# Where a weight-splitting step stands between the products of a sequence mixer, and at the start of an MLP

## The chip, the core and the metric

The kernel runs on one core of one Trainium2 chip. The metric is device time in microseconds (us), the median of several runs. The engines are TensorE (PE in the profile, its weight loads PEld), VectorE (DVE), ScalarE (ACT), GpSimd (POOL) and SyncE (SP); SyncE and ScalarE also issue DMAs from their own queues, in their program's order.

## The reference

Two layers of the same kind run one after the other on x (2048 tokens, 576 features). Each layer is a Fourier mixing and then an MLP (576 to 4608 to 576), both behind two layer norms and with a residual:

```python
def _A_ref(x, dft_seq_re, dft_seq_im, dft_hid_re, dft_hid_im):
    a = jnp.einsum("bsd,ed->bse", x, dft_hid_re)
    b = jnp.einsum("bsd,ed->bse", x, dft_hid_im)
    return jnp.einsum("ts,bse->bte", dft_seq_re, a) - jnp.einsum("ts,bse->bte", dft_seq_im, b)

def _B_ref(x, w1, b1, w2, b2):
    h = _gelu(jnp.einsum("bsd,df->bsf", _layernorm(x), w1) + b1)
    return jnp.einsum("bsf,fd->bsd", h, w2) + b2

x = x + _A_ref(_layernorm(x), ...)
x = x + _B_ref(_layernorm(x), ...)
# and both once more
```

Both layers use the same matrices.

## The kernel before

All large products are done in a 2x2 block scheme with seven block products in the place of eight (numbered 1 to 7, run in `ORDER`, 1, 6, 2, 5, 7, 3, 4). To keep fp32 accuracy each operand is split into a high part (fp32r) and a low part (the rest), and each product is three passes, high x high, high x low, low x high. A high part is a ScalarE copy (`activation` with Copy), a low part a VectorE subtraction of it from the source; L201 is the helper `sub`, L198 the helper `add`.

**Sequence** multiplies along the tokens: sixteen t blocks, of which the first two are done in `first_mms` and the other fourteen (t = 2 to 15) in `run`, seven products of 24 matmuls (128x288) each, 98 product steps. In product step n the program issues `low` of step n + 2 on VectorE, `high` of step n + 3 on ScalarE, the 24 matmuls, and `post`, which takes the finished bank away (ScalarE for products 1, 2, 5 and 7, VectorE for 6, 3 and 4, after 4 also the transpose L208; after 7 GpSimd does two adds). `sums(t + 1)` makes two sums of the blocks of the next t on VectorE: `tmp` = block 2 + block 3, and block 2 - block 0. The blocks come in by SyncE's DMAs from `in_cs`, in the order 0, 2, 3, 1, each as a ring buffer falls free (`load_c`). `low` of product 1 also rewrites block 0 (L704), and the next `high`, that of product 6, reads what it wrote.

**The weights' background.** `weights()` is a generator that splits the first MLP matrix, in 18 quarters of seven weight steps. Weight step n is `high(n)` (two ScalarE copies, L284 and L285), `low(n)` (a 128x384 VectorE subtraction, and in four of the seven steps a GpSimd add or subtraction), and `keep(n)`: the store to `w1_parts` and, in four of the seven, the load of the next piece (SyncE). Three stage buffers go round. The Sequence of the first layer advances the generator with `pump()` twice behind a product, and it issues the store on ScalarE's queue there; the MLP's first half goes on with it (`BEHIND` lists at which positions of a group), and its stores are SyncE's.

**MLP** runs over the two halves of the tokens. `inner(q)` makes seven products of seven matmuls (128x512) for one of 18 pieces of the hidden features, `outer` multiplies back (128x288); a group g is two inner runs and the outer products of the group before. `advance()` counts positions in a group and runs what is due there. In the first half of the first layer `make(g)` splits the second MLP matrix beside it; its steps are `one`, `six`, `five`, `three`, `seven`, `four` and `two`, each a ScalarE copy of the high part (L1169) and a VectorE low part (128x576) with the store behind it. Group 0 has no outer products: its positions 0 to 6 are the second half of `inner(0)`, 7 to 13 are `inner(1)`.

All three engines run in program order, and the order is written by hand: there is no scheduler.

Of the kernel before, what the change touches and what calls it, by code (L numbers as in the profile page):

```python
# [15 lines left out]
P = 128  # L16
NT = S // P
DH = D // 2
NP = NT // 2
NQ = F // P // 2  # L20
NG = NQ // 2
# [41 lines left out]
EARLY_X = (12800, 9344, 8192)  # L63
EARLY_T = 10496
BEHIND = (0, 2, 2, 4, 5, 6, 15, 16, 16, 17, 17, 19, 21, 21)
H_AT = (8704, 22400)
C2_AT = (OWN_AT, 37760)
Y_AT = (RN - Y_N, 0)
# [92 lines left out]
def spectral_mixer(ctx: ExitStack, tc: tile.TileContext, x, dh, c0, cs, w1, b1, w2, b2, out):  # L161
# [35 lines left out]
    def add(engine, dst, a, b, op=OP.add):  # L197
        engine.tensor_tensor(dst, a, b, op=op)  # L198
# [65 lines left out]
    def weights():  # L264
        b = raw(4, 3 * P)
        a22, a21, a11, a12 = (b[:, k] for k in range(4))
        g = nc.gpsimd
        steps = ((4, a22, lambda: add(g, a22, a21, a22)), (1, a11, lambda: sub(g, a21, a11, a21)),
                 (5, a22, lambda: sub(g, a11, a22, a11)), (2, a12, lambda: sub(g, a12, a12, a11)),
                 (6, a11, None), (7, a21, None), (3, a12, None))  # L270

        def load(q, k):
            if q < NQ:
                dma(b[:, k], w1[q][:, k])

        def at(n):
            return stage(3, 5 * P)[:, n % 3]

        def cut(a):
            return a.rearrange("p (k f) -> p k f", f=P)  # L280

        def high(n):
            src, t = cut(steps[n % 7][1]), cut(at(n))
            nc.scalar.activation(t[:, 1:4:2], src[:, 0:3:2], AF.Copy)  # L284
            nc.scalar.activation(t[:, 2], src[:, 1], AF.Identity, bias=power[:, 2:3], scale=middle)  # L285

        def low(n):

            q, k = divmod(n, 7)
            i, src, then = steps[k]  # L290
            t = cut(at(n))
            sub(nc.vector, t[:, 0:5:2], cut(src), t[:, 1:4].bitcast(F32))
            if then:
                then()

        def keep(n):

            q, k = divmod(n, 7)
            stores[0].dma_start(w1s[q, steps[k][0] - 1], at(n).bitcast(F32))
            if k in (2, 4, 5, 6):  # L300
                load(q + 1, {2: 0, 4: 2, 5: 1, 6: 3}[k])
            if k == 6:
                made[0] = q + 1

        for k in range(4):
            load(0, k)
        for _ in range(4):
            yield
        high(0)
        for n in range(7 * NQ):  # L310
            yield
            low(n)
            if n + 1 < 7 * NQ:
                high(n + 1)
            yield
            keep(n)
        stage.free()
        raw.free()

# [10 lines left out]
    class Sequence:  # L330
# [354 lines left out]
        def block(self, t, k):  # L685
            return self.live[t, k](NP, P)

        def sums(self, t):
            add(nc.vector, self.tmp(NP, P), self.block(t, 2), self.block(t, 3))
            sub(nc.vector, self.block(t, 2), self.block(t, 2), self.block(t, 0))  # L690

        def source(self, t, i):
            return self.tmp(NP, P) if i == 5 else self.block(t, {1: 0, 6: 0, 2: 1, 7: 2, 3: 1, 4: 3}[i])
# [64 lines left out]
        def run(self, hidden):  # L758
# [12 lines left out]
            for n, (t, i) in enumerate(steps):  # L771
                self.load_c()
                if n and n + 2 < len(steps):
                    self.low(*steps[n + 2])
                if n % 7 == 2 and t + 1 < NT:
                    self.sums(t + 1)
                self.load_c()
                if n + 3 < len(steps):
                    self.high(*steps[n + 3])
                self.mms(t, i)  # L780
                if n == 1:
                    self.first_turn(0, outs[0])
                    hidden.reserve()
                self.post(t, i)
                if n == 1:
                    self.first_post(1, outs[1])
                if n == 3:
                    self.first_turn(1, outs[1])
                if t == NT - 1:
                    hidden.begin(self, ORDER.index(i))  # L790
                if n == 3 and not self.early:
                    dma(b1t, b1)
                if n % 7 != 2 and n > 3 and (t < NT - 1 or n % 7 < 4):
                    pump()
                    pump()
            for k in range(2):
                self.L[k].free()
# [323 lines left out]
    def mlp(hid, store, first, ends, before, after):  # L1121


        half, X, Y = hid.half, hid.X, hid.Y
        stores[0] = nc.sync
        xv, y = X(2, NP, DH), Y(7, 5, TC)
        U = Block(A, U_AT[half], 4 * DH)
        uv = U(4, DH)
# [65 lines left out]

        def advance(to=None):
            at[1] += to is None
            for _ in range(BEHIND.count(at[0]) if to is None and group[0] else 0):
                pump()
            while kept and kept[0][0] <= at[1]:
                kept.pop(0)[1]()  # L1200
            while due and due[0][0] <= (at[0] if to is None else to):
                due.pop(0)[1]()
            at[0] += 1
# [176 lines left out]
        for k in range(4 * first):  # L1380
            load_raw(0, k)
        for g in range(NG + 1):
            at[0], group[0] = 0, g or not first
            if first and not g:
                soon, late = make(0)
                due.extend((n, step) for n, (_, step) in zip((3, 4), soon))
            elif first:
                due.extend(late)
                if g < NG:
                    soon, late = make(g)  # L1390
                    due.extend(soon)
# [117 lines left out]
```

## Time and profile before

| | |
|---|---|
| median of 3 runs | 2625.3 us (2624.54 to 2627.97) |
| the profiled execution | 2624.75 us, span 2623.0 us |
| busy: TensorE, weight loads, VectorE, ScalarE, GpSimd | 2614.4, 2466.3, 1836.8, 1120.2, 791.5 us |
| first layer's Sequence, products | about 60 to 378 us of the span |
| first layer's MLP, first half | from about 440 us |
| second layer's Sequence | about 1320 to 1700 us |

Times in the trace are us from the start of the span. An engine's row gives start, length, engine, line, operation, what it writes and reads with the sizes, a count where neighbours are merged, and in brackets the idle time before it and what ended it. TensorE's row in the page counts pipelined matmuls, so its 100% says that it is seldom empty, not that it runs at its best pace.

### The profile page before, as it was taken

What the parts mean: (1) busy time and instruction counts of PE and PEld (TensorE: products, weight loads), DVE (VectorE), ACT (ScalarE), POOL (GpSimd) and SP (SyncE); (2) the same over time, 40 slices, a digit from 0 to 9 for tenths busy, and PEclk for the clock granted to TensorE, in tenths of its full rate; (3) what the DMA queues carried; (4) which work ended last, traced back from release to release, by engine and by line L of the source; (5) the groups of instructions that cost most, each with busy time, mean ns of one, the idle gap of its engine ahead of it and who ended that gap; (6) DMA issues with size and microseconds to landing.
All of it is one profiled execution on the core that took longest, in us unless ns stands there. A gap on an engine that the chain in (4) does not pass through costs nothing.

```text
span 2623.0 us, 44794 instructions
## 1 busy us (share of the span) xinstructions
PE 2614.4 (100%) x17252; PEld 2466.3 (94%) x17252; DVE 1836.8 (70%) x2580; ACT 1120.2 (43%) x1821; POOL 791.5 (30%) x638
## 2 busy tenths in 40 slices
PE   9999999999999999999999999999999999999999
PEld 9999999899999989998999999999999999899998
DVE  8999987778787765556687776576555557655555
ACT  7555555555553443333354333353333325433332
POOL 5334333544444332222251000132122233322222
PEclk9999999999999999999999999999999999999999
DMA  6667676778788666676544343756666685666664
GB/s 226 223 236 234 234 255 215 266 278 301 279 299 300 178 202 195 194 222 210 173 175 135 122 124 124 211 159 194 193 195 194 195 268 169 199 195 195 194 194 155
DMA packets 223238, 544.91 MB, mean 208 GB/s; under 512 B 23712, under 2 KB 74912, under 8 KB 222880
## 3 DMA queue, kind: packets, MB, share of 16 engines
q1 hardware_dynamic: 210496, 513.91, 62.2%
q10 hardware_dynamic: 12528, 28.12, 2.8%
q8 instruction: 137, 2.24, 0.3%
q14 instruction: 77, 0.63, 0.1%
HBM read 429.87 MB, written 114.72 MB: 208 GB/s over the span
## 4 chain that ended last, share of the span: by engine, by line
PE 92%; DVE 5%; DMA 1%; issue 1%; POOL 1%; ACT 0%; DVEq 0%; ACTq 0%; SPq 0%; POOLq 0%
PE bank L211 91%; DVE R L201 3%; DVE A L201 1%; DMA w_parts<-R 1%; DMA A<-in_cs 0%; PE bank L991 0%; DVE A L198 0%; PE bank L1035 0%; DVE moments L242 0%; PE bank L994 0%; ACT R L698 0%; DMA A<-in_w 0%; DMA R<-w_parts 0%; PE bank L1045 0%; POOL A L198 0%
## 5 line engine op out<-in xcount | busy, mean ns | idle before, releaser
L211 PE MATMUL bank<-R 128*128 128x288 f32 (+2 forms) x16972 | 2585.9, 314 | 3.9 <-DVE R L201 1.2
L211 PEld LDWEIGHTS bank<-R 128*128 128x128 f32 x16972 | 2434.8, 189 | 150.8 <-DVE R L201 4.3
L198 DVE TENSOR_TENSOR A<-bank,A 128x576 f32<-128x576 f32 (+3 forms) x812 | 567.6, 707 | 510.2 <-PE bank L211 457.7
L201 POOL TENSOR_TENSOR R<-A,R 128x512 fp32r<-128x512 f32 (+1 forms) x292 | 380.0, 1310 | 912.4 <-ACT R L1299 560.6
L201 DVE TENSOR_TENSOR R<-A,R 128x1024 fp32r<-128x1024 f32 (+10 forms) x534 | 535.0, 1028 | 34.6 <-ACT R L698 14.3
L1299 ACT ACTIVATE R<-A 128x512 fp32r<-128x512 f32 x288 | 177.5, 630 | 356.4 <-DVE A L201 219.5
L198 POOL TENSOR_TENSOR A<-A 128x576 f32<-128x576 f32 (+2 forms) x102 | 155.0, 1527 | 531.1 <-ACT A L743 338.9
L1234 ACT ACTIVATE bank<-bank,b1t 128x512 f32<-128x512 f32 (+1 forms) x224 | 144.9, 647 | 350.5 <-DVE bank L198 233.6
L698 ACT ACTIVATE R<-A 128x1024 fp32r<-128x1024 f32 x196 | 205.6, 1054 | 123.8 <-PE bank L211 61.0
L198 DVE TENSOR_TENSOR bank<-bank,A 128x512 f32<-128x512 f32 (+1 forms) x228 | 152.3, 670 | 147.7 <-PE bank L211 147.0
L201 POOL TENSOR_TENSOR A<-A 128x288 f32<-128x288 f32 (+3 forms) x152 | 190.3, 1255 | 198.1 <-DVE R L201 103.6
L201 DVE TENSOR_TENSOR A<-A 128x1024 f32<-128x1024 f32 (+3 forms) x166 | 163.5, 989 | 6.2
L201 DVE TENSOR_TENSOR R<-bank,R 128x512 fp32r<-128x512 f32 x232 | 156.1, 676 | 5.5 <-ACT R L1299 5.0
L1299 ACT ACTIVATE R<-bank 128x512 fp32r<-128x512 f32 x216 | 121.0, 595 | 33.9 <-PE bank L211 33.9
L201 DVE TENSOR_TENSOR A<-bank,A 128x512 f32<-128x512 f32 x144 | 98.1, 681 | 0.4
L1261 ACT ACTIVATE A<-bank 128x512 f32<-128x512 f32 (+1 forms) x76 | 43.7, 575 | 120.2 <-PE bank L211 120.1
L284 ACT ACTIVATE R<-A 128x256 fp32r<-128x256 f32 x126 | 51.9, 412 | 63.7 <-DMA w_parts<-R 27.1
L1234 ACT ACTIVATE A<-bank,b1t 128x512 f32<-128x512 f32 (+1 forms) x76 | 50.5, 665 | 63.4 <-DVE bank L198 63.4
L232 POOL TENSOR_TENSOR moments<-moments,power 128x1 f32<-128x1 f32 x32 | 25.5, 797 | 134.9 <-DVE moments L234 117.5
L285 ACT ACTIVATE R<-A,power,middle 128x128 fp32r<-128x128 f32 x126 | 60.6, 481 | 0.0
L258 ACT ACTIVATE A<-A,moments 128x576 f32<-128x576 f32 x58 | 49.3, 867 | 23.7 <-DMA A<-x_mid 11.7
L198 DVE TENSOR_TENSOR A<-A 128x1024 f32<-128x1024 f32 x28 | 35.8, 1277 | 20.0 <-DMA A<-in_cs 12.3
(70 smaller groups left out, 612.9 us busy)
## 6 DMA issues: line engine op xcount, KB each, us to landing
R<-w_parts SPq DMA_DIRECT2D x504, 320.0 KB, 3.4
R<-w_parts SPq DMA_DIRECT2D x189, 576.0 KB, 3.7
A<-in_cs SPq DMA_DIRECT2D x112, 512.0 KB, 4.5
w_parts<-R SPq DMA_DIRECT2D x63, 576.0 KB, 6.2
w_parts<-R ACTq DMA_DIRECT2D x75, 320.0 KB, 4.3
w_parts<-R SPq DMA_DIRECT2D x51, 320.0 KB, 4.9
uv_mid<-A SPq DMA_DIRECT2D x28, 576.0 KB, 5.4
A<-in_w SPq DMA_DIRECT2D x72, 192.0 KB, 5.4
```

The costliest lines, as they stand in the source:

```text
L198: engine.tensor_tensor(dst, a, b, op=op)
L201: engine.tensor_tensor(dst, a, b, op=OP.subtract)
L211: nc.tensor.matmul(o, a, b, start=start, stop=stop, skip_group_check=True)
L232: nc.gpsimd.tensor_tensor(mv[:, 3:4], mv[:, 2:3], power[:, 0:1], op=OP.pow)
L258: nc.scalar.activation(dst, src, AF.Identity, bias=mv[:, 4:5], scale=mv[:, 3:4])
L284: nc.scalar.activation(t[:, 1:4:2], src[:, 0:3:2], AF.Copy)
L285: nc.scalar.activation(t[:, 2], src[:, 1], AF.Identity, bias=power[:, 2:3], scale=middle)
L698: nc.scalar.activation(self.cells[t, i](2, NP, P)[:, 0], self.source(t, i), AF.Copy)
L1234: nc.scalar.activation(dst, src, AF.Gelu_apprx_tanh, bias=bias(f))
L1261: nc.scalar.activation(up, o, AF.Copy)
L1299: nc.scalar.activation(H[q, k](2, TC)[:, 0], src, AF.Copy)
```

## The change

Three edits, which move work and leave all computation as it is.

1. `weights()` in the Sequence: `keep(n - 1)` and `high(n)` come first, then `low(n)`. `run` pumps once ahead of the product's matmuls (store of the step before, high part) and once behind `post` (low part). Before, both pumps stood behind `post`, and the second issued `low(n)` with `high(n + 1)`. In the MLP (two entries in `stores`) it goes on as before.
2. `sums(t + 1)`: one sum behind the low part of the fourth product step of a block, one at the fifth, instead of both at the third. The step without a pump is the seventh of a block instead of the third.
3. MLP, first half of the first layer: `five` and the high part of `six` of `make(0)` move from positions 0 to 2 of group 1 to 8, 11 and 12 of group 0, the low part of `six` from 3 to 0 of group 1; group 1 pumps 12 times (`BEHIND_1`) instead of 14.

```diff
+BEHIND_1 = (0, 2, 2, 4, 15, 16, 16, 17, 17, 19, 21, 21)
...
-        high(0)
+        done = 0
         for n in range(7 * NQ):
+            if n:
+                keep(n - 1)
+            if done == n:
+                high(n)
+                done += 1
             yield
             low(n)
-            if n + 1 < 7 * NQ:
+            if len(stores) > 1 and n + 1 < 7 * NQ:
                 high(n + 1)
+                done += 1
             yield
-            keep(n)
+        keep(7 * NQ - 1)
...
-                if n % 7 == 2 and t + 1 < NT:
-                    self.sums(t + 1)
+                if n % 7 in (3, 4) and t + 1 < NT:
+                    self.sums(t + 1, (n % 7 - 3,))
                 self.load_c()
                 if n + 3 < len(steps):
                     self.high(*steps[n + 3])
+                step = n % 7 != 6 and n > 3 and (t < NT - 1 or n % 7 < 5)
+                if step:
+                    pump()
                 self.mms(t, i)
...
-                if n % 7 != 2 and n > 3 and (t < NT - 1 or n % 7 < 4):
-                    pump()
+                if step:
                     pump()
...
-        stores[0] = nc.sync
+        stores[:] = nc.sync, nc.sync
...
-            for _ in range(BEHIND.count(at[0]) if to is None and group[0] else 0):
+            for _ in range((BEHIND if group[0] > 1 else BEHIND_1).count(at[0]) if to is None and group[0] else 0):
...
-            at[0], group[0] = 0, g or not first
+            at[0], group[0] = 0, g if first else NG
...
-                due.extend((n, step) for n, (_, step) in zip((3, 4), soon))
+                due.extend((n, step) for n, (_, step) in zip((3, 4, 8, 11, 12), soon + late[:3]))
+                late = [(0, late[3][1]), *late[4:]]
```

(`sums` gets an argument that says which of its two instructions to issue. Line numbers of the changed kernel are 1 higher in the helpers, L202 for L201, and up to 11 higher further on.)

VectorE in one t block of the first Sequence, from the low part of product 7 to that of the next block's product 6, before. R<-A,R 128x1024 is a low part, 128x3x128 a weight step's low part, A<-A the sums and the rewriting of block 0, A<-bank,A `post`:

```order
L201 TENSOR_TENSOR R<-A,R 128x1024
L198 TENSOR_TENSOR A<-A 128x1024
L201 TENSOR_TENSOR A<-A 128x1024
L201 TENSOR_TENSOR R<-A,R 128x1024
L201 TENSOR_TENSOR R<-A,R 128x3x128
L201 TENSOR_TENSOR R<-A,R 128x1024
L201 TENSOR_TENSOR R<-A,R 128x3x128
L201 TENSOR_TENSOR R<-A,R 128x1024
L201 TENSOR_TENSOR A<-A 128x1024
L198 TENSOR_TENSOR A<-bank,A 128x288
L201 TENSOR_TENSOR R<-A,R 128x3x128
L201 TENSOR_TENSOR R<-A,R 128x1024
```

The same place after the change, from the weight step behind that first low part on:

```order
L202 TENSOR_TENSOR R<-A,R 128x3x128
L202 TENSOR_TENSOR R<-A,R 128x1024
L199 TENSOR_TENSOR A<-A 128x1024
L202 TENSOR_TENSOR R<-A,R 128x3x128
L202 TENSOR_TENSOR R<-A,R 128x1024
L202 TENSOR_TENSOR A<-A 128x1024
L202 TENSOR_TENSOR R<-A,R 128x3x128
L202 TENSOR_TENSOR R<-A,R 128x1024
L202 TENSOR_TENSOR A<-A 128x1024
L199 TENSOR_TENSOR A<-bank,A 128x288
L202 TENSOR_TENSOR R<-A,R 128x3x128
L202 TENSOR_TENSOR R<-A,R 128x1024
```

The two sums have moved down, each behind a low part, and a weight step has come in above them.

ScalarE around the sixth product step of a block, before: `high` of product 1 of the next block, `post` of product 7, a store, a weight step's two copies, and L698 again, `high` of product 6; the pair behind that one is of the weight step whose low part comes a product later:

```order
L698 ACTIVATE R<-A 128x1024
L743 ACTIVATE A<-bank 128x288
L299 DMA w_parts<-R 128x640
L284 ACTIVATE R<-A 128x2x128
L285 ACTIVATE R<-A,power,middle 128x128
L698 ACTIVATE R<-A 128x1024
L299 DMA w_parts<-R 128x640
L284 ACTIVATE R<-A 128x2x128
L285 ACTIVATE R<-A,power,middle 128x128
L698 ACTIVATE R<-A 128x1024
```

After; here each pair belongs to the weight step whose low part stands in the same product step:

```order
L707 ACTIVATE R<-A 128x1024
L300 DMA w_parts<-R 128x640
L285 ACTIVATE R<-A 128x2x128
L286 ACTIVATE R<-A,power,middle 128x128
L752 ACTIVATE A<-bank 128x288
L707 ACTIVATE R<-A 128x1024
L300 DMA w_parts<-R 128x640
L285 ACTIVATE R<-A 128x2x128
L286 ACTIVATE R<-A,power,middle 128x128
L707 ACTIVATE R<-A 128x1024 x2
```

The pair and the store stand ahead of `post` instead of behind it, and the pair is one weight step less ahead of VectorE.

GpSimd at the start of group 1 of the MLP (128x576 is a subtraction of `six`, 128x384 a weight step's, 128x512 the low parts of the hidden activations), before:

```order
L201 TENSOR_TENSOR A<-A 128x576
L198 TENSOR_TENSOR A<-A 128x384
L201 TENSOR_TENSOR R<-A,R 128x512 x2
L201 TENSOR_TENSOR A<-A 128x384
L201 TENSOR_TENSOR R<-A,R 128x512 x2
```

And after:

```order
L202 TENSOR_TENSOR A<-A 128x576
L199 TENSOR_TENSOR A<-A 128x384
L202 TENSOR_TENSOR A<-A 128x384
L202 TENSOR_TENSOR R<-A,R 128x512 x4
L202 TENSOR_TENSOR A<-A 128x576
```

The second weight step's subtraction now stands ahead of all four low parts instead of between them.

More of the change, by code (lines that the diff above doesn't have):

```diff
@@ L686, in block, with sums @@
             return self.live[t, k](NP, P)
-        def sums(self, t):
-            add(nc.vector, self.tmp(NP, P), self.block(t, 2), self.block(t, 3))
-            sub(nc.vector, self.block(t, 2), self.block(t, 2), self.block(t, 0))
+        def sums(self, t, which=(0, 1)):
+            if 0 in which:
+                add(nc.vector, self.tmp(NP, P), self.block(t, 2), self.block(t, 3))
+            if 1 in which:
+                sub(nc.vector, self.block(t, 2), self.block(t, 2), self.block(t, 0))
         def source(self, t, i):
```

## The prediction

> **What bounds the kernel now.** I read the page, then the windows of a few stages, then who waited for whom on VectorE and TensorE, then the chain and the timeline around the waits that TensorE pays for. First the page: its span, its TensorE line, and the chain that ended last by line.
>
> ```profile
> span 2623.0 us, 44794 instructions
> PE 2614.4 (100%) x17252; PEld 2466.3 (94%) x17252; DVE 1836.8 (70%) x2580; ACT 1120.2 (43%) x1821; POOL 791.5 (30%) x638
> PE bank L211 91%; DVE R L201 3%; DVE A L201 1%; DMA w_parts<-R 1%; DMA A<-in_cs 0%; PE bank L991 0%; DVE A L198 0%; PE bank L1035 0%; DVE moments L242 0%; PE bank L994 0%; ACT R L698 0%; DMA A<-in_w 0%; DMA R<-w_parts 0%; PE bank L1045 0%; POOL A L198 0%
> ```
>
> TensorE is never idle for long, so no edit of order can win more than the little that TensorE loses. To price that loss I need the pace of an undisturbed stage. Windows of the second layer's Sequence, of the first layer's, and of the first MLP groups (columns: stretch, its length, then busy time and count by engine; a second question gave the last row, from the first matmul of one product to the first of the same product eleven t blocks later):
>
> ```profile
> 1320.00:1700.00 380.00, 380.00 (x2875) 380.00 (x2874) 271.32 (x286) 156.06 (x201) 60.73 (x59) 1.00 0.47 149
> 60.20:142.70 82.50, 82.50 (x626) 82.50 (x625) 78.98 (x76) 44.58 (x79) 25.65 (x16) 1.00 0.65 214
> 463.50:501.00 37.50, 35.59 (x192) 30.32 (x192) 29.90 (x44) 21.29 (x42) 17.81 (x15) 1.00 0.70 237
> 85.60:334.55 248.95, 247.33 (x1851) 245.16 (x1850) 236.59 (x231) 141.73 (x257) 93.47 (x61) 1.00 0.70 235
> ```
>
> The pace is 380 / 2875 = 0.1322 us a matmul, so a product of 24 takes 3.17 us and a t block of seven 22.2 us. Eleven blocks are 1848 matmuls, 244.3 us at that pace; they took 248.95, so the first Sequence loses 4.6 us, all after 142.7 (626 x 0.1322 = 82.8 before it, nothing lost). In the same eleven blocks VectorE is busy 236.59 us, 21.5 us a block, and it is never ahead: what is left are these waits (engine and line, waited for, us in total, times, longest), from 61 to 345 us, twelve blocks:
>
> ```profile
> DVE R L201 <- ACT R L698: 4.1, 12, 0.8
> DVE A L198 <- DVE R L201: 3.7, 5, 0.8
> DVE A L198 <- issue: 3.2, 2, 2.1
> DVE A L198 <- DMA A<-in_cs: 1.0, 1, 1.0
> ```
>
> It waits for TensorE nowhere. The lower three rows are one wait, that of the first of the two sums (`tmp` = block 2 + block 3) for block 3's DMA: 7.9 us, 0.66 a block. A block costs VectorE 21.5 + 0.3 (first row) + 0.66 and the pipeline's own gaps, 22.6 us, against TensorE's 22.2: **in this stage VectorE sets the pace**, and TensorE's loss is the difference.
>
> In the MLP groups the window above has TensorE idle 37.50 - 35.59 = 1.9 us, nearly all before three rows of its timeline:
>
> ```profile
> 474.16 5.77 PE L211 MATMUL bank<-R 128*128 128x512 f32 x36 [0.56 <-DVE bank L198]
> 480.74 18.84 PE L211 MATMUL bank<-R 128*128 128x288 f32 x109 [0.81 <-POOL R L201]
> 499.98 5.21 PE L211 MATMUL bank<-R 128*128 128x512 f32 x32 [0.41 <-DMA R<-w_parts]
> ```
>
> Everything that the change can win is 4.6 + 1.9 = 6.5 us, 0.25%. About 0.2%, 5.2 us, is what a measurement of this kernel can tell from no change.
>
> **The change, part by part.** *Sums moved (Sequence, behind the fourth and fifth product instead of the third).* Instructions and DMAs are the same. The block that the first sum waits for gets 3.2 us more, one product and a low part, against waits of at most 2.1 us: -7.9 us of VectorE's time over twelve blocks. In the second layer the same move is free: there VectorE has 380 - 271 = 109 us to spare.
>
> *A weight step's high part moved into the step of its own low part.* Before, `low(n)` found its high part made one product earlier. Now step n's two ScalarE copies (L284, L285) come in the same product step, behind `high` of the Sequence and ahead of `post`. Where this costs is the sixth product's step: there ScalarE's queue starts with `high` of the next block's i=6, whose source VectorE has only just written (L704, the second row of VectorE below). ScalarE's timeline, then VectorE's, at one such step before:
>
> ```profile
> 150.37 1.06 ACT L698 ACTIVATE R<-A 128x1024 fp32r<-128x1024 f32 x1 [4.76 <-DVE A L201]
> 151.34 0.40 ACT L284 ACTIVATE R<-A 128x256 fp32r<-128x256 f32 x1
> 151.64 0.48 ACT L285 ACTIVATE R<-A,power,middle 128x128 fp32r<-128x128 f32 x1
> 147.04 2.04 DVE L201 TENSOR_TENSOR R<-A,R 128x1024 fp32r<-128x1024 f32 x1
> 149.11 1.23 DVE L201 TENSOR_TENSOR A<-A 128x1024 f32<-128x1024 f32 x1
> 150.25 0.45 DVE L198 TENSOR_TENSOR A<-bank,A 128x288 f32<-128x288 f32 x1
> 150.62 0.55 DVE L201 TENSOR_TENSOR R<-A,R 128x384 fp32r<-128x384 f32 x1
> 151.46 1.94 DVE L201 TENSOR_TENSOR R<-A,R 128x1024 fp32r<-128x1024 f32 x1 [0.29 <-ACT R L698]
> ```
>
> Before, the weight's low part (128x384) goes at 150.62 and the i=6 low part at 151.46, as soon as its high part is there. After, the 128x384 one must wait for L285, which ends at 152.12; it starts there, VectorE stands still from 150.70 to about 152.15 (1.45 us), and the i=6 low part starts 0.47 later, at 152.62 instead of 151.46: 1.16 us later, in every block. Twelve blocks: +13.9 us. Queued behind the waiting instruction are that low part, `post` and the transpose; TensorE's product i=6 waits for the first. The Trainium skill, "TensorE: Matmul & The Clock Gate", the table at its head, gives ScalarE's queue as strict FIFO; the rows agree (nothing passes the copy that waited 4.76 us), and by that rule L284 can't slip ahead. No sum here needs it.
>
> At the third product's step VectorE has one low part between two weight steps (1.14 us from start to start, as from 149.11 to 150.25). ScalarE needs a store's issue, L284 and L285 between the two; the issue took 0.33 us,
>
> ```profile
> 195.14 0.33 ACTq L299 DMA_DIRECT2D w_parts<-R  x1
> ```
>
> and L284's start to L285's end 0.78 (151.34 to 152.12), together 1.1: a wait of 0 to 0.15 us a block, I take 0. The weight step that left the seventh product moved to the third, and one step more falls in the whole Sequence (77 low parts for 76): 0.55 us in the last block, where VectorE has room.
>
> *Stores on ScalarE's queue* now go before `post`'s copies, one product step after their low part as before; SyncE's weight loads follow the block loads of the step instead of preceding them, by about a product at most, and the three stage buffers now have two steps between a store and the next writer. I cost this at nothing: what hides it is TensorE's 3.17 us a product; if that cover goes, it comes out as more of the wait above (below, the third rival).
>
> So VectorE's time in the Sequence changes by +13.9 - 7.9 = +6.0 us, and TensorE, which VectorE holds, by as much less what the first blocks absorb, in which VectorE still had a lead (no loss before 142.7): about one block's 1.16. I take **+5.0**. Bounds: -4.6, if the whole loss goes, and +7.8, with nothing absorbed and 0.15 a block on top.
>
> *MLP.* Two weight-splitting steps of `make(0)` go from the start of group 1 (positions 0 to 2) into group 0 (8, 11, 12), and group 1 runs one weight step less before its outer products. VectorE there, before (start, length):
>
> ```profile
> 463.52 0.70 DVE L198 TENSOR_TENSOR bank<-bank,A 128x512 f32<-128x512 f32 x1 [0.91 <-PE bank L211]
> 466.82 0.69 DVE L198 TENSOR_TENSOR A<-bank,A 128x512 f32<-128x512 f32 x1 [2.60 <-PE bank L211]
> 467.42 0.75 DVE L201 TENSOR_TENSOR R<-A,R 128x576 fp32r<-128x576 f32 x1
> 471.55 0.74 DVE L201 TENSOR_TENSOR R<-A,R 128x576 fp32r<-128x576 f32 x1
> 473.41 0.69 DVE L198 TENSOR_TENSOR bank<-bank,A 128x512 f32<-128x512 f32 x1
> ```
>
> The two 128x576 low parts land in gaps of 0.91 and 2.60 us, which hold them even if GpSimd slows them (an estimate: two thirds more, as the 2.04 us low part above against the 1.23 us add, is 1.25 us). Without both, the add that TensorE waited for at 474.16 (473.41 to 474.10) comes some 1.2 us sooner: that 0.56 is gone, and so is a small one before it. The 0.81 is GpSimd's, which runs in this order:
>
> ```profile
> 474.64 1.02 POOL L198 TENSOR_TENSOR A<-A 128x384 f32<-128x384 f32 x1 [0.78 <-DVE R L201]
> 475.62 2.87 POOL L201 TENSOR_TENSOR R<-A,R 128x512 fp32r<-128x512 f32 x2
> 478.44 1.01 POOL L201 TENSOR_TENSOR A<-A 128x384 f32<-128x384 f32 x1
> 479.41 2.52 POOL L201 TENSOR_TENSOR R<-A,R 128x512 fp32r<-128x512 f32 x2
> ```
>
> The 1.01 us add at 478.44 moves ahead of the low parts and its VectorE source comes earlier, so the third low part, which TensorE waits for, ends some 2 us sooner; TensorE arrives 0.7 sooner. I count this wait as gone too, with 0.2 left. The 0.41 at 499.98 stays: the load that ends it is queued on SyncE behind a store that waits for VectorE, and nothing there moves. Gain 1.9 - 0.4 = 1.5, and some restart time of the pipeline at three waits: **-1.8**. Bounds -2.4 and -0.5.
>
> **Sum.** +5.0 - 1.8 = +3.2 us. The profiled execution took 2624.75 us, 0.55 under the median of the runs, 2625.3: I predict 2625.3 + 3.2 = 2628.5. The bounds give 2618.3 and 2632.6.
>
> **Rivals.**
> *The lost time of VectorE is given back by GpSimd.* GpSimd's adds around the step shown:
>
> ```profile
> 145.03 2.96 POOL L201 TENSOR_TENSOR A<-A 128x288 f32<-128x288 f32 x2
> 151.30 1.02 POOL L201 TENSOR_TENSOR A<-A 128x384 f32<-128x384 f32 x1 [3.31 <-issue]
> ```
>
> VectorE's low parts beside them took 2.04 us (147.04) and 1.94 (151.46), its subtraction at 149.11, with GpSimd still, 1.23: each add costs VectorE about 0.7 us. An add that falls into the new 1.45 us standstill costs VectorE nothing. One a block gives back 12 x 0.7 = 8.4, the Sequence ends at 5.0 - 8.4 = -3.4, the kernel at 2625.3 - 3.4 - 1.8 = 2620.1. The Trainium skill, "SBUF — State Buffer", Who interferes with whom, has it that a VectorE instruction with two SBUF inputs contends with a GpSimd one that reads SBUF, by an exclusive lock; by that rule the gift could be the add's whole length. For it: the adds are there, about five a block by the code (four of seven weight steps have one, `post` has two). Against: the step's own add starts only behind the waiting low part. Chance 0.2.
> *The two moves cancel:* the standstill is as long as computed, but the three first blocks absorb theirs (3.5 us) and another 1.5 goes in blocks where block 3 came late by 2.1. Sequence 0, total 2623.5. Chance 0.2.
> *Slower, by one mechanism:* high and low part in one step leave a late high part no cover. From 105 to 333 us ScalarE's L284 waited for a landing store 15 times, 19.7 us:
>
> ```profile
> ACT R L284 <- DMA w_parts<-R: 19.7, 15, 2.7
> ```
>
> Then, that cost VectorE nothing. If a fifth of it now does, 4 us, the Sequence costs 9.0 and the kernel 2632.5; it decides, 5.2 us over before, once VectorE's waits for ScalarE pass 1.6 us a block. Against: the store is now issued a step further ahead of the next writer. Chance 0.18. The forecast itself has 0.42.
>
> **How the numbers follow.** Slower by over 0.2% (above 2630.5) is that last rival and a fifth of the forecast's own spread: 0.26. Faster by over 0.2% (under 2620.1) is half of the first rival and a little: 0.12. Within: 0.62. The range runs from the first rival to the last, 2620.0 to 2632.5, and leaves out about 0.1 at either end.
>
> **What would show it.** VectorE's waits from 61 to 345 us: the rows with `A L198` for `in_cs` gone; a new row, the 128x384 low part (`R L201`) for ScalarE's L286 (its new number), about 12 times and 1.4 us each. TensorE's loss in eleven blocks near 10 us, paid at i=6. No TensorE wait at 474 for VectorE, at most 0.2 for GpSimd near 479, the 0.4 for `w_parts` still there. I am wrong if that new wait is under 0.6 us a block, or if VectorE's busy time a block falls below 21 us.

## The result, and the profile after

The changed kernel takes 2629.36 us (median of 22 runs) against 2624.51 us for the kernel before (median of 22 runs on the same chip): the ratio is 1.0018, 95% interval 1.0012 to 1.0025. The change costs about 4.9 us, a fifth of a per cent. The profiled execution took 2629.45 us, its span is 2627.7 us, 4.7 us longer than before's 2623.0.

First the page of the changed kernel (span, and the chain that ended last, by line):

```profile
span 2627.7 us, 44766 instructions
PE bank L212 82%; DVE R L202 1%; DMA A<-uv_mid 1%; PE bank L1002 0%; POOL A L199 0%; PE bank L1046 0%; DMA A<-in_w 0%; DVE A L199 0%; PE bank L1005 0%; DMA A<-x_mid 0%; DMA w_parts<-R 0%; SPq L196 0%; DMA A<-in_c 0%; POOL A L202 0%; PE bank L1056 0%
```

TensorE still carries the chain. Since both kernels have the same 17252 matmuls in the same order, the two traces can be laid side by side matmul by matmul. How much later the same matmul starts in the changed kernel (worked out from the starts in both traces):

| place | after less before |
|---|---|
| first product of the first Sequence's `run` | +0.2 us |
| its last product (97 products on) | +4.4 us |
| a matmul of the hidden product behind it, at 404 us of before | +6.0 us |
| a matmul of group 1 of the MLP, at 531 us of before | +3.6 us |
| the second layer's Sequence, from 1391 us of before | +4.7 us |
| last matmul | +4.7 us |

So the Sequence costs 4.2 us, the passage behind it 1.6, the MLP's start gives 2.5 back (6.03 to 3.57 us), and about 1.0 is lost at the start of the second layer. Of the last, 0.8 us sits before one matmul, at 1348.6 us, which waits for a ScalarE copy; ScalarE had waited 6.45 us for a load shortly before. No code differs there; a loss of 0.5 to 0.9 us at this place is in five of the thirteen profiles taken and not in the other eight. It is left out of what follows, and what decides it stays open.

Windows over the same 97 products in both kernels, before and then after (length, then busy time and count of TensorE, weight loads, VectorE, ScalarE, GpSimd):

```profile
60.23:372.95 312.72, 311.05 (x2330) 308.64 (x2329) 294.75 (x288) 175.42 (x313) 110.76 (x72) 1.00 0.69 231
```

```profile
60.41:377.37 316.96, 310.11 (x2331) 308.25 (x2329) 285.85 (x288) 172.33 (x313) 103.56 (x72) 1.00 0.63 226
```

97 products at 3.173 us are 307.8 us, so TensorE lost 4.9 us before and loses 9.2 us after. VectorE issues the same 288 instructions. Its idle time grew from 312.72 - 294.75 = 18.0 to 31.1 us, by 13.1; its busy time fell by 8.9. Both have to be explained. What VectorE waited for, 61 to 345 us, after:

```profile
DVE R L202 <- ACT R L286: 11.5, 11, 1.8
DVE R L202 <- issue: 5.2, 6, 1.5
DVE R L202 <- POOL A L199: 3.3, 2, 1.8
DVE R L202 <- ACT R L707: 1.7, 2, 0.9
DVE R L202 <- POOL A L202: 1.5, 1, 1.5
```

The sums' waits for `in_cs` are gone. All rows but the fourth are waits of one kind of instruction, the weight step's 128x384 low part, 21.5 us in 20 waits. (The profile puts some of them down to `issue` or GpSimd, which had been done for long; ScalarE's copy ended last in each.) Eleven of them are 1.45 to 1.51 us long and stand at the sixth product step of each block, a twelfth at 358 us; two are 1.79 us, at 121 and 282 us; the rest are small. One of the twelve, on VectorE and ScalarE, and what TensorE makes of it:

```profile
129.62 0.45 DVE L199 TENSOR_TENSOR A<-bank,A 128x288 f32<-128x288 f32 x1
131.57 1.69 DVE L202 TENSOR_TENSOR R<-A,R 128x384 fp32r<-128x384 f32 x2 [1.50 <-issue]
```

```profile
129.73 1.06 ACT L707 ACTIVATE R<-A 128x1024 fp32r<-128x1024 f32 x1 [5.71 <-DVE A L202]
130.70 0.40 ACT L285 ACTIVATE R<-A 128x256 fp32r<-128x256 f32 x1
131.00 0.48 ACT L286 ACTIVATE R<-A,power,middle 128x128 fp32r<-128x128 f32 x1
```

```profile
133.32 0.94 PE L212 MATMUL bank<-R 128*128 128x288 f32 x5 [1.73 <-DVE R L202]
```

VectorE is free at 130.07 and starts the weight's low part at 131.57, when L286 is through. L286 sits behind `high` of product 6 (L707), which stood 5.71 us waiting for VectorE. Product 6 then waits 1.73 us for its own low part, which is queued behind. TensorE does not pay in every block: it paid in six of the eleven, at 108.8, 133.3, 156.7, 269.2, 293.8 and 317.2 us, where VectorE had no lead left.

### The profile page after: what moved, and what is told of

Its sections match the earlier page's. It is cut to its first block, busy times and chain, and to the rows that moved or that the text cites. A ratio compares the mean times of both kernels' runs of the same rounds, so it can differ in the third digit from the quotient of the medians.

```text
span 2627.7 us, 44766 instructions
## 1 busy us (share of the span) xinstructions
PE 2614.2 (99%) x17252; PEld 2466.2 (94%) x17252; DVE 1830.1 (70%) x2580; ACT 1117.4 (43%) x1821; POOL 782.7 (30%) x638
## 4 chain that ended last, share of the span: by engine, by line
PE 83%; DMA 1%; DVE 1%; POOL 1%; issue 0%; ACT 0%; SPq 0%; ACTq 0%; DVEq 0%; POOLq 0%
PE bank L212 82%; DVE R L202 1%; DMA A<-uv_mid 1%; PE bank L1002 0%; POOL A L199 0%; PE bank L1046 0%; DMA A<-in_w 0%; DVE A L199 0%; PE bank L1005 0%; DMA A<-x_mid 0%; DMA w_parts<-R 0%; SPq L196 0%; DMA A<-in_c 0%; POOL A L202 0%; PE bank L1056 0%
## 5 line engine op out<-in xcount | busy, mean ns | idle before, releaser
L202 POOL TENSOR_TENSOR R<-A,R 128x512 fp32r<-128x512 f32 (+1 forms) x292 | 379.9, 1309 | 915.8 <-ACT R L1310 558.8
L202 DVE TENSOR_TENSOR R<-A,R 128x1024 fp32r<-128x1024 f32 (+10 forms) x534 | 531.6, 1020 | 68.4 <-ACT R L707 23.0
L707 ACT ACTIVATE R<-A 128x1024 fp32r<-128x1024 f32 x196 | 204.3, 1053 | 146.1 <-DVE A L202 80.2
L202 POOL TENSOR_TENSOR A<-A 128x288 f32<-128x288 f32 (+3 forms) x152 | 185.5, 1224 | 196.6 <-DVE R L202 103.7
L202 DVE TENSOR_TENSOR A<-A 128x1024 f32<-128x1024 f32 (+3 forms) x166 | 162.5, 983 | 5.6 <-DVE A L202 0.5
L202 DVE TENSOR_TENSOR R<-bank,R 128x512 fp32r<-128x512 f32 x232 | 156.3, 677 | 5.6 <-ACT R L1310 5.0
L202 DVE TENSOR_TENSOR A<-bank,A 128x512 f32<-128x512 f32 x144 | 98.2, 682 | 0.4
L286 ACT ACTIVATE R<-A,power,middle 128x128 fp32r<-128x128 f32 x126 | 60.6, 481 | 0.0
L1180 ACT ACTIVATE R<-A 128x576 fp32r<-128x576 f32 x63 | 42.2, 676 | 16.6 <-DVE A L202 7.1
```

Of the source, the lines that this page charges most:

```text
L202: engine.tensor_tensor(dst, a, b, op=OP.subtract)
L707: nc.scalar.activation(self.cells[t, i](2, NP, P)[:, 0], self.source(t, i), AF.Copy)
L1180: nc.scalar.activation(got2[g, i](2, 2, DH)[:, :, 0], src, AF.Copy)
```

## The experiments

Each number is a median; before is 2624.44 us in the session of e1 to e4, 2624.74 in that of e5 to e9 and 2624.67 in that of e10 to e12, each on another chip. TensorE's loss in the Sequence is the length of the window over the same 97 products, less 307.8 us.

| kernel | us | ratio to before, 95% | Sequence window, loss |
|---|---|---|---|
| after | 2629.36 | 1.0012 to 1.0025 | 9.2 |
| e1_sums_only | 2621.50 | 0.9981 to 0.9998 | 0.6 |
| e2_weight_first | 2620.61 | 0.9974 to 0.9992 | 2.5 |
| e3_high_ahead | 2619.36 | 0.9971 to 0.9989 | 1.0 |
| e4_mlp_as_before | 2630.98 | 1.0016 to 1.0034 | 10.3 |
| e5_tail | 2629.37 | 1.0010 to 1.0028 | 10.0 |
| e7_sums_undone | 2637.81 | 1.0035 to 1.0062 | 19.9 |
| e8_ahead_and_tail | 2620.43 | 0.9973 to 0.9990 | 1.3 |
| e9_sums_and_mlp | 2620.02 | 0.9973 to 0.9990 | 0.9 |
| e10_loads_early | 2629.56 | 1.0010 to 1.0028 | 10.7 |
| e11_ahead_and_loads | 2618.71 | 0.9969 to 0.9986 | 0.0 |
| e12_no_weight_adds | 2618.64 | 0.9967 to 0.9985 | 0.1 |

**e1: the sums alone, in the kernel before.**

```diff
-                if n % 7 == 2 and t + 1 < NT:
-                    self.sums(t + 1)
+                if n % 7 in (3, 4) and t + 1 < NT:
+                    self.sums(t + 1, (n % 7 - 3,))
```

> The kernel before with one edit: the two sums go behind the fourth and fifth product, nothing else moves. Theory (VectorE sets the pace of the first Sequence): the 7.9 us that VectorE waited for block 3 in twelve blocks go, it gets ahead of TensorE (21.5 + 0.3 us a block against 22.2), and TensorE's loss in eleven blocks falls from 4.6 us to under 1.5; time 2624.5 - 3.5 = about 2621. Rival (GpSimd): the time won is spent where GpSimd's adds overlap VectorE's low parts, the loss stays at 3 to 5 us; time 2623.5 to 2625.

2621.5 us, 2.9 under before. The window over the 97 products:

```profile
60.62:369.01 308.39, 308.16 (x2331) 307.93 (x2330) 284.42 (x288) 177.43 (x313) 111.05 (x72) 1.00 0.67 235
```

308.39 against 312.72 us: the Sequence gains 4.3 us, nearly all that it had lost. VectorE now waits for TensorE:

```profile
DVE A L198 <- PE bank L211: 6.3, 6, 1.6
```

That row was not there before. So VectorE had set the pace, as the theory says, and no longer does. But two things changed at once: the sums' waits of 7.9 us are gone, and VectorE's busy time fell by 10.3 us, which fits neither theory. How much of the gain is the waits' alone this run does not show (e7 returns to it). (The profile of this kernel has a wait of 1.6 us for `w_parts` at 677 us in the MLP, and three of the others have a shorter one, 0.6 to 0.9 us, at 685 to 719 us.)

**e2: the weight's copies ahead of `high` of product 6.**

```diff
+                if step and n % 7 == 5:
+                    pump()
                 if n + 3 < len(steps):
                     self.high(*steps[n + 3])
-                if step:
+                if step and n % 7 != 5:
                     pump()
```

> The kernel after with one edit: at the sixth product step of a block the store and the weight step's two ScalarE copies are issued ahead of the Sequence's high part instead of behind it, into the 4.4 to 6.4 us in which ScalarE waits there for VectorE. Theory: VectorE's eleven waits of 1.45 to 1.5 us for L286 are gone and the first Sequence loses under 2 us instead of 9; time 2629.4 - 7 = about 2622. Rival 1 (stores and copies ahead of the product and of post are what delays): the waits go but the time stays within 1.5 us of 2629.4. Rival 2 (GpSimd): VectorE's busy time in the Sequence, which fell by 9.6 us with the standstills, comes back by 6 us or more, and half of the gain goes; time 2625 to 2626.

2620.61 us, 8.8 under after, with two instructions and a store moved one place up in ScalarE's queue, in one product step of seven. The window:

```profile
60.31:370.61 310.30, 309.00 (x2330) 308.07 (x2329) 286.77 (x288) 175.62 (x313) 101.77 (x72) 1.00 0.64 231
```

The Sequence loses 2.5 us for 9.2, a little over the 2 that was expected; ten of the eleven waits at the sixth product step are gone. Three longer waits are left: 1.8 and 2.6 us at 121 and 277 us, and 1.4 us at 329 us, at the sixth step, where the weight's copies wait 3.59 us for a late GpSimd addition. Rival 1 falls: stores and copies ahead of `post` stay in every other step. Rival 2 falls as well: VectorE's busy time is 286.77 us, 0.9 more than with the standstills, so nothing was taken back.

**e3: the high part a product ahead of its low part.**

```diff
-    background, stores = [], [nc.scalar]
+    background, stores = [], [nc.scalar, nc.scalar]
```

(with two entries `weights()` issues `low(n)` and then `high(n + 1)`, as in the kernel before)

> The kernel after with one edit: in the Sequence, too, a weight step's low part is followed by the next step's high part, a product ahead of its use, as in the kernel before; the pump ahead of the product then issues the store alone. Theory: as with the weight's copies issued first, no wait of VectorE for L286 is left, neither the eleven of 1.5 us nor the two of 1.8 us, and the first Sequence loses under 1.5 us; time about 2621. Rival 1 (the stores' and pumps' place is what costs): within 1.5 us of 2629.4. Rival 2 (GpSimd takes back): 2625.

2619.36 us, 5.1 under before: all of the change but this one reordering is a gain. The window:

```profile
60.08:368.90 308.82, 308.07 (x2330) 307.84 (x2329) 285.33 (x288) 175.07 (x315) 106.52 (x72) 1.00 0.65 232
```

The theory was off in one point: three longer waits for L286 stayed, of 1.9, 2.1 and 1.3 us at 120, 275 and 327 us (the last behind a copy that waits 4.01 us for a landing store). TensorE lost 0.9 us at the first and nothing at the others; e10 and e11 go after it.

**e4: the MLP edit undone, in the kernel after.**

```diff
-(BEHIND if group[0] > 1 else BEHIND_1).count(at[0])
+BEHIND.count(at[0])
-zip((3, 4, 8, 11, 12), soon + late[:3]))
-                late = [(0, late[3][1]), *late[4:]]
+zip((3, 4), soon))
```

> The kernel after with its MLP edit undone: make(0)'s steps stand at positions 0 to 3 of group 1 again, and group 1 pumps 14 times. Theory: TensorE's waits at 471 to 481 us come back (0.3 + 0.7 + 1.0 us and restarts), 2.4 us; time 2629.4 + 2.4 = about 2631.8. Rival: those waits came from how far the Sequence had got, not from the place of the steps, and do not come back; time 2629.4 within 0.7.

2630.98 us, 1.6 over after where 2.4 was expected. TensorE's waits from 460 to 512 us in this kernel, and in the kernel after:

```profile
PE bank L212 <- DVE bank L199: 0.6, 1, 0.6
PE bank L212 <- POOL R L202: 0.3, 1, 0.3
PE bank L212 <- DVE A L199: 0.2, 1, 0.2
```

```profile
PE bank L212 <- DVE R L202: 0.3, 1, 0.3
```

The waits come back with the steps' old place, only GpSimd's is shorter than before's 0.8, and that for `w_parts` stays away. In this kernel, too, the delay against before falls between 404 and 531 us, from 5.9 to 4.9 us. So 1.1 of the 2.5 us that the MLP's start gave back come without the edit, as the rival has it; by which cause is not shown.

**e5: one weight step fewer at the Sequence's end**, in the kernel after.

```diff
-(t < NT - 1 or n % 7 < 5)
+(t < NT - 1 or n % 7 < 4)
-(BEHIND if group[0] > 1 else BEHIND_1).count(at[0])
+BEHIND.count(at[0])
```

> The kernel after with one weight step fewer at the end of the first Sequence (its last block pumps behind products 1 to 4 of ORDER instead of 1 to 5; group 1 of the MLP pumps 14 times for it). Theory (the 1.6 us that TensorE lost at 387 to 390 us come from the last steps' stores and loads, which share saturated DMA engines with dh_mid's loads): they go, time 2629.4 - 1.6 = about 2627.8. Rival: the loads are late because of their place on SyncE or of the later end of the Sequence alone; time within 0.5 of 2629.4. A second rival: the two more pumps in group 1 bring its waits at 471 to 481 us back, 2629.4 to 2630.5.

2629.37 us, no change. But the place is the right one: between the Sequence's end and the hidden product the delay against before stays at 6.1 us, where in after it grows from 4.4 to 6.0. In the kernel after, TensorE has two waits there,

```profile
388.16 1.33 PE L212 MATMUL bank<-R 128*128 128x288 f32 x8 [0.26 <-DVE R L202]
389.82 2.38 PE L212 MATMUL bank<-R 128*128 128x288 f32 x16 [0.33 <-DVE R L202]
```

which this kernel has not. They come behind ScalarE's copies that wait for a load, in after from 370 to 390 us (1.5 us in two such waits in this kernel):

```profile
ACT R L890 <- DMA R<-dh_mid: 5.5, 4, 2.7
```

The DMA engines are full in that stretch of after (two windows; the last columns are the clock, the DMA share and GB/s), and less so from 378 us in this kernel (third row) and at the same place of before (fourth):

```profile
372.00:378.00 6.00, 6.00 (x47) 6.00 (x47) 3.11 (x4) 3.99 (x7) 2.01 (x2) 1.00 1.06 356
378.00:384.00 6.00, 6.00 (x47) 6.00 (x46) 5.89 (x9) 2.57 (x4) 0.00 (x0) 1.00 1.06 332
378.00:384.00 6.00, 6.00 (x48) 6.00 (x47) 5.96 (x9) 4.71 (x7) 0.67 (x1) 1.00 0.87 312
373.00:379.00 6.00, 6.00 (x47) 6.00 (x47) 5.89 (x9) 4.95 (x8) 0.00 (x0) 1.00 0.73 226
```

The second rival took the gain: with 14 pumps in group 1 the MLP's start gives back 1.3 us instead of 2.5. The weight step costs about as much in the one place as in the other.

**e7: the sums back at the third product step**, in the kernel after (the diff of e1 reversed).

> The kernel after with the sums moved back: both behind the low part at the third product step, the weights' order and the MLP as in after. Theory (what VectorE waits for adds up): the 7.9 us of waits for block 3 and the slower low parts of before (about 10 us of busy time) come on top of the eleven standstills; VectorE had no slack, so the Sequence gets 8 to 18 us longer; time 2637 to 2647. Rival: the standstills, ahead of the sums in the block, give block 3 its time to land, so nothing adds; time within 2 us of 2629.4.

2637.81 us, 8.5 over after, inside the range. The window:

```profile
60.56:388.23 327.67, 314.10 (x2330) 310.19 (x2329) 286.59 (x287) 172.19 (x313) 108.82 (x72) 0.99 0.63 220
```

The size comes out by the waits alone (VectorE idles 10.0 us more); the 10 us of busy time that the theory added did not come. And TensorE does not wait for VectorE mostly, but for ScalarE's `post`:

```profile
PE bank L212 <- ACT A L748: 10.4, 11, 2.3
PE bank L212 <- DVE R L202: 3.1, 5, 1.1
```

One of the eleven, on ScalarE:

```profile
286.29 0.33 ACTq L300 DMA_DIRECT2D w_parts<-R  x1
286.72 0.42 ACT L285 ACTIVATE R<-A 128x256 fp32r<-128x256 f32 x1 [4.40 <-DVE R L202]
287.04 0.48 ACT L286 ACTIVATE R<-A,power,middle 128x128 fp32r<-128x128 f32 x1
287.43 0.39 ACT L748 ACTIVATE A<-bank 128x288 f32<-128x288 f32 x1
```

The store, now ahead of `post`, waits for a low part that stands behind both sums on VectorE; ScalarE stands still for 4.40 us, and `post` (L748), which needs nothing of all this, comes behind it. TensorE waits 1.86 us for that `post`. So the first edit of the change needs the second one: without it, it costs 8.5 us more. The second does not need the first (e1).

**e8: e3 and e5 together.**

> The kernel after with two edits: the weight's high part is made a product ahead of its low part again (as in e3_high_ahead, 2619.4), and one weight step fewer at the Sequence's end (as in e5_tail). Theory: the 0.4 us that the former still lost at 380 us go, the MLP's start stays as it is there; time about 2619.0. Rival: the 14 pumps of group 1 bring its waits back, 2620.5 to 2621.5.

2620.43 us, nearer to the rival. Two edits that were worth 10.0 and 0 us alone are worth 8.9 together, which is the same within the intervals.

**e9: the sums and the MLP edit, in the kernel before** (the weights' order of before, 14 pumps in group 1).

> The kernel before with two of the change's three edits: the sums moved, and make(0)'s steps moved into group 0 (group 1 still pumps 14 times, since the Sequence makes one weight step less). The weights' order and the pumps' places are those of before. Theory (gains of separate stages add): 2621.5 of the sums alone less the 2 us that the MLP edit was worth in after, about 2619.5. Rival: with 14 pumps in group 1 the MLP edit saves less than 0.7 us; 2621.

2620.02 us, between the two. TensorE's wait for GpSimd in group 1 is still there,

```profile
PE bank L211 <- POOL R L201: 0.7, 1, 0.7
```

so the MLP edit is worth 1.5 us here by the medians (2621.50 - 2620.02, of two sessions, with intervals that overlap), and leaves this wait.

**e10: the loads of the weight pieces ahead of the block loads**, in the kernel after.

```diff
             if then:
                 then()
+            if early[0] and k in (2, 4, 5, 6):
+                load(q + 1, {2: 0, 4: 2, 5: 1, 6: 3}[k])
+                loaded.add(n)
```

(`keep` then leaves these loads out; `early` is cleared where the MLP begins)

> The kernel after with one edit: in the Sequence the load of a weight's next piece is issued on SyncE right behind the low part that frees it, ahead of the next product step's block loads, instead of with the store behind them. Theory (the loads' place on SyncE, which the prediction costed at nothing, makes the weight pieces late: at 102 to 112 us one sits behind a block load that waits for its buffer, lands at 118, and GpSimd, ScalarE and VectorE wait in turn, 1.8 us at 121 and again at 282): the two waits of 1.8 us go, the eleven of 1.5 us stay, and the Sequence loses about 4 us less than 9; time 2629.4 - 3.6 = about 2626. Rival: SyncE now waits for VectorE's low part ahead of the block loads, the blocks come later, and the time stays within 1 us of 2629.4 or rises.

2629.56 us: a miss. The cause named was right and its worth was not. Both waits of 1.79 us are gone, and GpSimd's add at 119 us starts 3.4 us sooner, at 115.5. But the window shows no gain:

```profile
60.44:378.94 318.50, 310.36 (x2330) 308.38 (x2329) 290.15 (x288) 172.17 (x313) 108.25 (x72) 1.00 0.63 224
```

VectorE idles 28.4 us for 31.1, and is busy 290.15 for 285.85: the 2.7 us that it waits less come back as 4.3 us of longer instructions, and GpSimd's busy time rises with it by 4.7.

**e11: e3 and e10 together.**

> The kernel after with two edits: the weight's high part a product ahead of its low part (as in e3_high_ahead, 2619.4), and the loads of the weight's pieces ahead of the block loads (as in e10_loads_early). Theory: the stall of 0.9 us that the former had left at 121 us goes; time about 2618.5, the fastest of all. Rival: nothing is left to win in the Sequence and the median stays within 0.5 us of 2619.4.

2618.71 us, the fastest version that computes everything, 0.22% under before (interval 0.14 to 0.31). The window is at TensorE's pace, with nothing lost:

```profile
60.37:368.20 307.83, 307.83 (x2331) 307.83 (x2329) 288.25 (x288) 174.96 (x315) 111.80 (x72) 1.00 0.66 233
```

Against e3's 2619.36 the intervals overlap; the stall of 0.9 us at 121 us is gone.

**e12: GpSimd's adds of the weight steps left out of the Sequence**, in the kernel after.

```diff
-            if then:
+            if then and len(stores) > 1:
```

> The kernel after without GpSimd's adds of the weight steps in the Sequence (44 instructions, left out, so that the first MLP weights of these steps are not the reference's). Theory (GpSimd's additions slow VectorE's instructions with two SBUF inputs): VectorE's 128x1024 low parts over 1.4 us, 17 of 96, become fewer than 7 (those beside the two adds of post stay), its busy time in the Sequence falls by 6 to 10 us, and with it TensorE's loss, though the standstills of 1.5 us stay; time 2629.4 - 6 = about 2623. Rival: the low parts' length has another cause; busy time within 2 us, and only the two waits of 1.8 us that came through GpSimd go; time about 2626.

2618.64 us, 10.7 under after where 6 was expected. The window:

```profile
60.13:368.02 307.89, 307.89 (x2331) 307.88 (x2329) 265.95 (x288) 176.50 (x313) 35.32 (x28) 1.00 0.65 235
```

Groups by shape, 61 to 345 us (count, then busy time and mean ns), of after and of this kernel:

```profile
L202 DVE TENSOR_TENSOR R<-A,R 128x1024 fp32r<-128x1024 f32 x86 | 116.4, 1353 | 1.7 <-ACT R L707 1.7
L202 DVE TENSOR_TENSOR R<-A,R 128x384 fp32r<-128x384 f32 x67 | 48.3, 721 | 22.3 <-ACT R L286 11.5 <-issue 5.2 <-POOL A L199 3.3
```

```profile
L202 DVE TENSOR_TENSOR R<-A,R 128x1024 fp32r<-128x1024 f32 x90 | 112.3, 1248 | 1.7 <-ACT R L707 1.7
L202 DVE TENSOR_TENSOR R<-A,R 128x384 fp32r<-128x384 f32 x71 | 40.0, 564 | 20.0 <-ACT R L286 18.9
```

VectorE is busy 19.9 us less, twice the upper figure of the theory. Of its 96 low parts of 128x1024, 5 are over 1.4 us long, for 17 in after, as the theory said. TensorE loses nothing although VectorE still waits 18.9 us for L286 (four waits of 1.45 us and one of 2.0, the others shorter, and more of them). A standstill costs nothing on an engine that has slack to take it.

## Why the prediction was right, and where only its sum was

Predicted 2628.5 us, range 2620.0 to 2632.5; measured 2629.36. The likeliest case, slower by the standstill with a gain in the MLP, is the one that came. Part of the nearness is luck. The forecast stood on a base of 2625.3 us from three runs, where 22 runs give 2624.51: the change is 4.9 us, and 3.2 was predicted. By the traces it is +4.2 in the Sequence for +5.0, +1.6 behind it and about +1.0 in the second layer for nothing, and -2.5 at the MLP's start for -1.8.

- *The standstill* (predicted +13.9 us of VectorE's time): the mechanism is shown, with twelve waits of 1.45 to 1.51 us at the place named, behind the instruction named, paid at i=6. e2 takes all but one away by moving two copies and a store up and saves 8.8 us, 6.7 of them in the Sequence (9.2 to 2.5). That is half of the 13.9: in five of the eleven blocks TensorE did not wait. By the Trainium skill, "TensorE: Matmul & The Clock Gate", the table at its head, ScalarE's queue is strict FIFO; in 129.73 to 131.47 us above it is, nothing passes the copy that waits.
- *The sums* (-7.9): not one of their waits is left. e1 alone gains 4.3 us in the Sequence, the whole loss but 0.6, with 10.3 us less of busy time beside it; e7 puts the waits back into the changed kernel at nearly the same busy time, and the Sequence gets 10.7 us longer.
- *The third product step* (0 to 0.15 us a block, taken as 0): at its bound at most. The small waits of the 128x384 low part, at all places, are 21.5 - 16.2 - 3.6 = 1.7 us, 0.14 a block.
- *Stores and loads at nothing*: this step failed, twice. At 102 to 113 us a weight piece's load sits on SyncE behind a block load, and VectorE's two waits of 1.79 us come of it (e10 takes them away, though the time stays). And the steps that moved into the last block put their stores and loads before `dh_mid`'s, which costs 1.6 us behind the Sequence (e5). The cover that the prediction named, TensorE's 3.17 us a product, was not there: behind the Sequence the DMA engines were full, and SyncE's queue stood still for over ten us at a block load:

```profile
102.27 0.33 SPq L196 DMA_DIRECT2D A<-in_w  x1
113.00 0.33 SPq L196 DMA_DIRECT2D A<-in_cs  x1
```

- *VectorE's busy time as before*: this step failed too, by the prediction's own sign of being wrong. Eleven blocks take 229.35 us of VectorE, 20.85 a block, under the 21 that was set as its limit (and TensorE's 253.48 us there are 9.2 over the 244.3 of its pace, near the 10 that was named):

```profile
85.81:339.29 253.48, 246.63 (x1851) 244.77 (x1849) 229.35 (x231) 138.26 (x255) 86.85 (x61) 1.00 0.64 231
```

So the term VectorE +6.0 us was made up otherwise: 13.1 us more idle, 8.9 less busy, 4.2 in sum, and TensorE's +4.2 lies near the +5.0 by two errors of opposite sign, which is luck. Of the 13.1 us, 12.7 add up from the waits: 17.7 for twelve standstills, 3.6 and 1.7 for the other waits of that low part, less the sums' 7.9 and 2.4 for waits on the Sequence's own high part.
- *The first rival* (GpSimd gives VectorE's lost time back) was right in the cause and the size, 8.4 us, and wrong in the place. Of the 8.9 us that the busy time fell, 8.7 are less waiting for GpSimd; the last section has the count. But the standstills are not needed for it: e1 and e3, which have none or one shorter one at the sixth step, are busy 284.42 and 285.33 us. Which neighbours meet depends on the whole order, and the order of before was the worst of all (294.75 us; the other complete versions 284.4 to 290.2). What in it brings more of them together was not found.
- *The third rival* (late high parts): its sign, waits of VectorE for ScalarE over 1.6 us a block, was passed, with 23.2 us in twelve blocks. But 16.2 of these are the standstills, and ScalarE's waits for a landing store, which were to be the cause, fell. From 61 to 345 us, before and then after:

```profile
ACT R L284 <- DMA w_parts<-R: 21.1, 17, 2.7
ACT R L285 <- DMA w_parts<-R: 8.9, 10, 1.5
```

In two blocks a high part did come late, through a load, 3.6 us of waits; e10 shows that without them the time is the same.
- *MLP* (-1.8, bounds -2.4 and -0.5): the waits named are gone, but not all by the edit. The trace has -2.5, and 1.1 of that came in e4 without the edit; by e4's median the edit is worth 1.6, near the 1.8. The waits at 474 and 480 us are gone, GpSimd's without the 0.2 that was left for it. That at 499.98 for `w_parts`, which was to stay, is gone too, also in e4, so the edit is not what removed it; 0.31 at 503.6 us for VectorE stands in its place. One reading of the prediction does not fit its own figures: a low part of 1.25 us is longer than the gap of 0.91 us that was to hold it.

## What to carry to other kernels

Where two engines run one after the other in program order, making an operand in the step that uses it can put a far wait into the nearer engine's path: look at what stands ahead of the producer in its queue, and issue the independent copy ahead of the one that will wait (e2: 8.8 us for one place in a queue). Price a standstill on the engine that sets the pace at its full length less its lead, and on one with slack at nothing. And the busy time of an engine can hold waits: compare instructions of one shape with and without a neighbour on the other engine before taking their length for work. A store or load that is moved has to be read against the queue that it lands in and against the traffic of that stretch, not against the length of a product.

## What was not expected of the hardware

GpSimd's additions cost VectorE twice what was expected of e12. There GpSimd does 103.56 - 35.32 = 68.2 us less and VectorE, with the same 288 instructions, takes 285.85 - 265.95 = 19.9 us less: 0.29 us of VectorE for each us of GpSimd. GpSimd's additions and subtractions over 128x384 take 1.01 us at the least and up to 2.00 in the kernel after, so its side is slowed too.

The traces also show how the two take turns. Before, at 140 us, VectorE's rows and then GpSimd's:

```profile
139.82 1.23 DVE L201 TENSOR_TENSOR A<-A 128x1024 f32<-128x1024 f32 x1
140.96 2.03 DVE L201 TENSOR_TENSOR R<-A,R 128x1024 fp32r<-128x1024 f32 x1
```

```profile
140.00 1.92 POOL L198 TENSOR_TENSOR A<-A 128x384 f32<-128x384 f32 x1 [14.14 <-DMA A<-in_w]
141.99 1.87 POOL L201 TENSOR_TENSOR A<-A 128x384 f32<-128x384 f32 x1
```

VectorE's first row has its usual 1.23 us. GpSimd's first row starts inside it and ends 0.87 us after its end; VectorE's second starts inside that one and ends 1.07 us after its end, and so on. Over the 97 products of all thirteen kernels the 128x1024 instructions that do not start beside a GpSimd one take 1.18 to 1.23 us, also where one starts later (316 times); of the 433 that do, 425 end 1.07 to 1.18 us after GpSimd's end. For 128x384 it is 0.51 to 0.56 us, and 0.40 to 0.43 us after that end in 271 of 281. GpSimd's 128x384 ones take 1.01 to 1.03 us in the 72 cases that start by themselves, and end 0.84 to 0.90 us after VectorE's end in 444 of the 456 that start beside it. So the one that starts second waits for the end of the other's instruction, and the profile counts the wait as busy time. VectorE's additions over 128x288 that read one operand from a bank are not touched: 0.44 to 0.46 us beside a GpSimd instruction, 0.41 to 0.46 otherwise.

This accounts for VectorE's busy time. The lengths of its instructions in the 97 products add up to 311.1 us before and 302.8 after (neighbours overlap a little, so this is more than the busy time). What those beside GpSimd take over the median of the others is 41.8 us in 66 instructions before, 33.1 in 56 after, 31.6 in e1, 37.5 in e10 and 9.8 in e12. Without it 269.3 us are left before, 269.7 after, and 268.6 to 270.1 in all thirteen.

The Trainium skill, "SBUF — State Buffer", Who interferes with whom, has a VectorE instruction with two SBUF inputs and a GpSimd one that reads SBUF contend, by an exclusive lock; the ends counted above agree. And a shorter wait was worth nothing in e10, since there VectorE waits 4.4 us more for GpSimd (33.1 to 37.5).
